# Sixteen weight tiles and eleven operand tiles begin at other places in a partition

## The chip, the cores and the metric

The kernel runs on one core of one Trainium2 chip. The metric is the device time of one execution in microseconds (us). A profiled execution also has a span, from its first to its last recorded instruction, and a trace of every instruction.

## What is computed

The inputs are q, k and v of shape 8 x 8 x 576 x 64 (batch, heads, sequence, head dimension), w_in (512 x 2048) and w_out (2048 x 512). q, k and v are float32; w_in and w_out arrive as 8-byte floats, which the kernel takes apart into two words.

```
q_s = softmax of q over the head dimension
k_s = softmax of k over the sequence
kv  = einsum('bhsd,bhse->bhde', k_s, v)
x   = einsum('bhsd,bhde->bhse', q_s, kv), heads put side by side: 4608 x 512
h   = x @ w_in
g   = h / (1 + exp(-1.702 h))
out = g @ w_out                                        4608 x 512, float32
```

## The kernel before

**Tiling.** The 4608 tokens are nine blocks of 512 (`t`, 0 to 8). For each block an attention part (`attend`) makes the block's x, transposed, with features on the partitions. A feed-forward part then goes through the 2048 hidden features in eight steps (`NS`) of two groups of 128 (`jj`); the pair `p` of groups goes up in even blocks and down in odd ones.

**Precision.** A matmul operand of the feed-forward part is kept as two float32r tiles, a high and a low part, and each product is three matmuls: high by high, high by low, low by high.

**First product, blocks 0 and 1** (`plain1`, line 795): for each step 24 matmuls of 512 columns, with `wj` (w_in) as the stationary operand and `xp` (x) as the moving one. **Blocks 2 to 8** (`ffn1`, line 842): seven products of six matmuls of 256 columns, in the order 6, 1, 2, 7, 5, 4, 3. They multiply sums of blocks of x (`xo`) by blocks of w_in (`wj`) or sums of these (`wt`); VectorE and ScalarE put the results together. That is 42 matmuls in a step. **Second product** (`ffn2`, line 905): 24 matmuls of 512 columns in a step, with the activated values `gh` and `gl` as the stationary operand and w_out (`w`) as the moving one, added up in four banks over the eight steps.

**Weights.** All sixteen tiles of w_out stay in SBUF from when they are converted (`load_w`, line 320, and `conv`, lines 329 to 369). Each of them is first the landing place (`raw`) of a piece of w_in, then of one of w_out, then holds the split w_out; four of them first hold v and q of block 0 (`early_tile`). w_in is split too and stored to memory (`kept`, `kept_t`), and from block 1 on GpSimd's DMA queue loads it back two steps ahead (`load_kept`, line 398): three DMAs a step, each issued when TensorE has read its buffer (`wj`, `wt`) for the last time. SP's queue carries everything else.

**Order.** `Plan` holds each piece of work with an engine, a cost and a rank, and writes out one fixed order per engine before anything runs. Costs and ranks don't depend on where a tile lies.

**Places.** All tiles come from one pool and lie one behind another in each partition in the order in which they are first named, behind a scratch for the descriptors of GpSimd's DMAs (16,384 bytes) and four constants of 32 bytes each. From the sizes it follows where a tile begins, in bytes modulo 512: `ident`, `kvn`, `g`, `gh`, `gl`, `tt`, `tmp` and `kt` at 128; the four `vt` (2,080 bytes each) at 128, 160, 192 and 224; `qt` and `qT` at 256; `wj`, `wide` and `wt` at 384; and, behind `first` with its 64 bytes, the sixteen tiles tagged `wo..` and the eleven tagged `place..` all at 448. Inside these tiles TensorE's operands begin at multiples of 512 from the tile's start, but those of `vt` (line 635) at multiples of 260. [...]

**The places of x.** Eleven tiles of 4 KB are shared: `xp` of block 0 is in 0 to 3 and of block 1 in 4 to 7; later `xf` is in 0 and 1, `xs` in 2 and 3, and `xo` of the products 7, 5, 4, 3, 6, 1, 2 in 4 to 10.

Of the kernel before, what the change touches and what calls it, by code (L numbers as in the profile page):

```python
# [9 lines left out]
F32 = mybir.dt.float32  # L10
F32R = mybir.dt.float32r
I32 = mybir.dt.int32
# [124 lines left out]
def efficient_attention_then_gelu_ffn(  # L137
# [27 lines left out]
    nc = tc.nc  # L165
    B, H, S, D = q.shape
    NTOK, DM = out.shape
    FF = w_out.shape[0]
    P = 128
    C = 4  # L170
# [6 lines left out]
    NS = NJ // 2  # L177
# [4 lines left out]
    SLOTS = 15  # L182
    Y, Z = 4, 5
    LATE = (0.0, 2.0, 6.0)

    const = ctx.enter_context(tc.tile_pool(name="const", bufs=1))
    psum = ctx.enter_context(tc.tile_pool(name="psum", bufs=1, space=bass.MemoryType.PSUM))
# [4 lines left out]

    def sb(name, shape, dtype=F32, tag=None):
        return const.tile(shape, dtype, name=name, tag=tag or name)

    ident = sb("ident", [P, P])
    kvn = [sb(f"kvn{i}", [P, NP, D]) for i in range(2)]
    gt = [[sb(f"g{i}{u}", [P, 2, HT]) for i in range(2 - u)] for u in range(2)]
    gs = [[sb(f"g{s}{i}", [P, 2, 2, HT], F32R) for i in range(2)] for s in "hl"]
    tt = sb("tt", [P, 4, HT])  # L200
# [27 lines left out]
    places = {}  # L228

    def place(n, name, shape, dtype=F32):  # L230
        if (n, name) not in places:
            places[n, name] = sb(f"{name}{n}", shape, dtype, tag=f"place{n}")
        return places[n, name]

    def xp(t, hp):
        return place(4 * t + hp, "xp", [P, 2, TB], F32R)

    def xf(half):
        return place(half, "xf", [P, 2, 2, HT])

    def xsum(n):
        return place(3 if n == 4 else 2, "xs", [P, 2, 2, HT])[:, n % 2]
# [63 lines left out]
    raws, wo = {}, {}  # L306

    def load_w(p, kind, rank):
        for jj in range(2):
            tag = f"wo{p}{jj}"  # L310

            def run(jj=jj, tag=tag, j=p + NS * jj):
                raw = raws[p, jj] = sb("raw", [P, 2 * DM], I32, tag=tag)
                if kind == "wi":
                    nc.sync.dma_start(
                        out=raw.rearrange("p (c f) -> p c f", c=KC),
                        in_=w_in[:, 2 * j * P : 2 * (j + 1) * P].rearrange("(c p) f -> p c f", p=P),
                    )
                else:
                    nc.sync.dma_start(out=raw, in_=w_out[j * P : (j + 1) * P, :])  # L320

            plan.add("SP", plan.ISSUE, (), (tag,), rank + 0.01 * jj, run, size=2 * DM * 4 * P)

    def words(raw):
        return raw.rearrange("p (f t) -> p f t", t=2)

    def high(f, w):

        nc.scalar.activation(f, w[:, :, 1].bitcast(F32), AF.Prelu, scale=2.0**-112, alpha=-(2.0**32))

    def narrow(f, w):

        fi = f.bitcast(I32)
        nc.vector.scalar_tensor_tensor(fi, fi, 3, w[:, :, 0], ALU.logical_shift_left, ALU.bitwise_or)

    def low(w):
        lo = w[:, :, 0].bitcast(U32)
        nc.vector.tensor_scalar(lo, lo, 29, None, ALU.logical_shift_right)  # L338
# [6 lines left out]
    def next_tmp(n):  # L345
        nt[n] += 1
        i = nt[n] % n
        return (tmp[i] if i < 2 else wide[:, i - 2]), ("tmp", i)

    def conv(p, kind, rank):  # L350

        for jj in range(2):
            ff, T = next_tmp(6)
            K = f"wo{p}{jj}"
            KD = K if kind == "wo" else ("wj", p % 2, jj)

            def w(jj=jj):
                return words(raws[p, jj])

            def dst(jj=jj):  # L360
                return wo[p, jj] if kind == "wo" else wj[p % 2][jj].rearrange("p s c f -> p s (c f)")

            def c5(jj=jj, ff=ff, tag=K, dst=dst):
                if kind == "wo":
                    wo[p, jj] = sb("w", [P, 2, DM], F32R, tag=tag)
                nc.scalar.copy(dst()[:, 0], ff)  # L366

            def c6(ff=ff, dst=dst):
                nc.vector.tensor_tensor(out=dst()[:, 1], in0=ff, in1=dst()[:, 0].bitcast(F32), op=ALU.subtract)  # L369

            plan.add("ACT", 0.66, (K,), (T,), rank, lambda ff=ff, w=w: high(ff, w()))
            plan.add("DVE", 0.38, (K,), (K,), rank, lambda w=w: low(w()))
            plan.add("DVE", 0.69, (K, T), (T,), rank, lambda ff=ff, w=w: narrow(ff, w()))
            plan.add("ACT", 0.62, (T,), (KD,), rank, c5)
            plan.add("DVE", 0.69, (KD, T), (KD,), rank, c6)
            if kind == "wi":

                def run_s(jj=jj):
                    nc.sync.dma_start(
                        out=kept[p][jj], in_=wj[p % 2][jj].bitcast(F32).rearrange("p s c f -> p (s c f)")  # L380
                    )

                plan.add("SP", plan.ISSUE, (KD,), (("kept", p, jj),), rank, run_s, size=2 * DM * P * 4)
# [72 lines left out]
    def late(t):  # L456

        return LATE[min(t, 2)]

# [23 lines left out]
    early = {}  # L483

    def early_tile(kind, hp):
        tag = f"wo{NS - 1 if kind == 'q' else NS - 2}{hp // 2}"
        if tag not in early:
            early[tag] = sb(f"early{tag}", [P, 2, 2, C * D], tag=tag)
        return early[tag][:, hp % 2].rearrange("p h (c d) -> p h c d", d=D), (("early", tag, hp % 2), tag)

    def load_v(b, hp, rank):
        if b == 0:
            x, K = early_tile("v", hp)
            src = v[b, 2 * hp : 2 * hp + 2, 0:SM, :]

            def run_e():
                nc.sync.dma_start(
                    out=x.rearrange("p h c d -> p h (c d)"), in_=src.rearrange("h (p c) d -> p h (c d)", c=CM)
                )

            plan.add("SP", plan.ISSUE, (), (K[0],), rank, run_e, size=2 * SM * D * 4)
            return

        def run():
            for h in range(2):
                nc.sync.dma_start(
                    out=vt[hp][:, h, :, 0:D], in_=v[b, 2 * hp + h, 0:SM, :].rearrange("(p c) d -> p c d", c=CM)
                )

        plan.add("SP", 2 * issue(b), (), (("vt", hp),), rank, run, size=3 * SM * D * 4, late=late(b))  # L510

    def load_q(t, hp, rank):
        runs = [(0, 1, 1), (1, 0, 1)] if hp % 2 else [(0, 0, 2)]
        x, K = early_tile("q", hp) if t == 0 else (None, (("qt", hp),))

        def run():
            for b, s0, p0, p1 in parts(t):
                for o, h, m in runs:
                    src = q[b, 2 * hp + h : 2 * hp + h + m, s0 : s0 + (p1 - p0) * C, :]
                    if t == 0:  # L520
                        nc.sync.dma_start(
                            out=x[p0:p1, o : o + m].rearrange("p h c d -> p h (c d)"),
                            in_=src.rearrange("h (p c) d -> p h (c d)", c=C),
                        )
                    else:
                        nc.sync.dma_start(
                            out=qt[hp][p0:p1, :, o : o + m], in_=src.rearrange("h (p c) d -> p c h d", c=C)
                        )

        plan.add(  # L530
            "SP", issue(t) * len(parts(t)) * len(runs), (), (K[0],), rank, run, size=(3 if t else 2) * TB * D * 4, late=late(t),
        )
# [81 lines left out]
    def kv_pairs(b, hps, t, rank):  # L614
# [5 lines left out]
        for hp in hps:  # L620
            reads += [("kt", hp), ("kl", hp), *(early_tile("v", hp)[1] if b == 0 else (("vt", hp),))]
# [383 lines left out]
```

## Time and profile before

| | |
|---|---|
| median of 2 runs | 851.38 us (851.37 to 851.38) |
| the profiled execution | 850.68 us, span 848.7 us |
| TensorE matmuls (PE) | 841.5 us busy, 99% of the span |
| TensorE weight loads (PEld) | 720.9 us, 85% |
| VectorE (DVE) | 520.8 us, 61% |
| ScalarE (ACT) | 496.5 us, 58% |
| GpSimd (POOL) | 116.4 us, 14% |
| DMA | 155.63 MB, mean 183 GB/s |

A matmul's record begins when the matmul begins and its end is modelled, so records of neighbours overlap: their mean length is not the pace. The pace is read from how far apart the beginnings lie, as the chain of waits does, whose pieces add up to the span. The row PEclk, the granted clock of TensorE in tenths of full speed, is 9 in all 40 slices of the page.

### The profile page before, as it was taken

To read this page: it belongs to the slowest core of one execution; us is meant where nothing else is said; L and a number is where in the kernel's file an instruction comes from. 1 tells how busy PE (TensorE), PEld (TensorE's weight loads), DVE (VectorE), ACT (ScalarE), POOL (GpSimd) and SP (SyncE) were. 2 spreads that over 40 slices of the span, in tenths; PEclk is the share of its full clock that TensorE was granted. 3 is DMA by queue.
4 is the path that set the end of the run, shared out by engine and by line. 5 is a ranking of instruction groups with operands and counts; after the bars stand their busy time and mean duration, and the time that the engine had idled before them with its cause. 6 is when DMAs were issued, how large, how long until landed. Compare 5 with 4: busy or idle time off the path is not lost.

```text
span 848.7 us, 14608 instructions
## 1 busy us (share of the span) xinstructions
PE 841.5 (99%) x5644; PEld 720.9 (85%) x5644; DVE 520.8 (61%) x1082; ACT 496.5 (58%) x839; POOL 116.4 (14%) x175
## 2 busy tenths in 40 slices
PE   9999999999999999999999999999999999999998
PEld 4687788778898898889988999899988998899996
DVE  8899995988637884456645674475357532453333
ACT  4798879769637667456744665564366533353222
POOL 1000021120114031110211021100110011101110
PEclk9999999999999999999999999999999999999999
DMA  9999935793469737564765476623664264416541
GB/s 289 287 347 353 265 133 190 238 327 151 134 213 234 216 81 230 163 196 112 230 191 147 131 210 186 174 88 124 194 182 122 68 210 150 145 50 199 174 149 51
DMA packets 127845, 155.63 MB, mean 183 GB/s; under 512 B 76576, under 2 KB 105760, under 8 KB 121376
## 3 DMA queue, kind: packets, MB, share of 16 engines
q0 software_dynamic: 25248, 83.37, 31.8%
q1 hardware_dynamic: 102528, 71.32, 28.4%
q8 instruction: 45, 0.74, 0.4%
q14 instruction: 24, 0.20, 0.1%
HBM read 128.45 MB, written 26.21 MB: 182 GB/s over the span
## 4 chain that ended last, share of the span: by engine, by line
PE 93%; DVE 3%; DMA 2%; ACT 1%; issue 1%; DVEq 0%
PE bank L905 44%; PE bank L842 33%; PE bank L795 8%; PE bank L635 2%; DMA raw<-in_moe_w_out 2%; PE bank L705 2%; PE bank L684 2%; PE bank L297 1%; PE bank L583 0%; PE bank L584 0%; DVE w L369 0%; DVE wj L369 0%; DVE gl L813 0%; DVE raw L338 0%; DVE kt L557 0%
## 5 line engine op out<-in xcount | busy, mean ns | idle before, releaser
L905 PE MATMUL bank<-w,gh 128*128 128x512 f32 x1152 | 359.3, 393 | 0.3 <-DVE w L369 0.3
L905 PE MATMUL bank<-w,gl 128*128 128x512 f32 x576 | 225.7, 392 | 0.0
L905 PEld LDWEIGHTS bank<-w,gh 128*128 128x128 f32 x1152 | 199.8, 188 | 30.2 <-DVE w L369 1.1
L842 PE MATMUL bank<-xo,wt 128*128 128x256 f32 x1344 | 187.6, 280 | 0.0
L842 PEld LDWEIGHTS bank<-xo,wt 128*128 128x128 f32 x1344 | 176.4, 188 | 11.0 <-DVE g L855 0.8
L842 PEld LDWEIGHTS bank<-xo,wj 128*128 128x128 f32 x1008 | 136.7, 188 | 12.2 <-issue 1.6
L842 PE MATMUL bank<-xo,wj 128*128 128x256 f32 x1008 | 145.7, 280 | 0.5 <-ACT tt L866 0.5
L858 ACT ACTIVATE g<-g 128x512 f32<-128x512 f32 x112 | 58.8, 525 | 142.6 <-DVE g L855 142.1
L905 PEld LDWEIGHTS bank<-w,gl 128*128 128x128 f32 x576 | 108.3, 188 | 24.0
L855 DVE TENSOR_TENSOR g<-bank,tt 128x256 f32<-128x256 f32 x168 | 70.7, 422 | 87.8 <-PE bank L842 87.5
L886 DVE TENSOR_TENSOR gl<-g,gh 128x512 fp32r<-128x512 f32 x112 | 77.2, 690 | 72.3 <-ACT gh L883 71.6
L855 DVE TENSOR_TENSOR tt<-bank,tt 128x256 f32<-128x256 f32 x112 | 47.3, 422 | 106.1 <-PE bank L842 88.8
L398 POOL DMA_DIRECT2D wj<-kept x96 | 59.4, 619 | 379.9 <-PE bank L842 321.4
L795 PE MATMUL bank<-xp,wj 128*128 128x512 f32 x384 | 100.6, 396 | 0.3 <-ACT wj L366 0.2
L795 PEld LDWEIGHTS bank<-xp,wj 128*128 128x128 f32 x384 | 71.0, 188 | 19.6 <-issue 2.6
L883 ACT CAST gh<-g 128x512 fp32r<-128x512 f32 x112 | 69.6, 621 | 3.2
L858 ACT ACTIVATE g<-bank 128x256 f32<-128x256 f32 x56 | 21.7, 387 | 73.5 <-PE bank L842 73.3
L546 POOL PARTITION_ALL_REDUCE mx<-mx x32 | 34.8, 1086 | 197.3 <-DVE mx L542 170.4
L398 POOL DMA_DIRECT2D wt<-kept_t x42 | 22.2, 530 | 124.0 <-PE bank L842 124.0
L858 ACT ACT_TABLE_LOAD x27 | 34.6, 1283 | 0.5
L665 ACT ACT_TABLE_LOAD x26 | 33.4, 1283 | 0.5
L866 ACT COPY tt<-bank 128x256 f32<-128x256 f32 x56 | 20.8, 371 | 19.1 <-PE bank L842 18.9
(103 smaller groups left out, 795.1 us busy)
## 6 DMA issues: line engine op xcount, KB each, us to landing
wt<-kept_t POOLq DMA_DIRECT2D x42, 1024.0 KB, 5.2
wj<-kept POOLq DMA_DIRECT2D x54, 512.0 KB, 3.7
wj<-kept POOLq DMA_DIRECT2D x42, 256.0 KB, 4.8
out<-tmp SPq DMA_DIRECT2D x36, 256.0 KB, 3.0
kt<-in_k SPq DMA_DIRECT2D x32, 256.0 KB, 4.0
raw<-in_moe_w_in SPq DMA_DIRECT2D x16, 512.0 KB, 8.2
raw<-in_moe_w_out SPq DMA_DIRECT2D x16, 512.0 KB, 7.4
kept<-wj SPq DMA_DIRECT2D x16, 512.0 KB, 7.1
```

Source lines behind the costliest of these rows:

```text
L398: "POOL", 1.0, (key,), (ring,), R(t, step - 2, off), lambda: nc.gpsimd.dma_start(out=out(), in_=src), size=size
L546: nc.gpsimd.partition_all_reduce(flat, flat, P, bass_isa.ReduceOp.max)
L635: nc.tensor.matmul(pk[r0 : r0 + D, m, cols], lhs, rhs, start=c == 0, stop=c == CM, tile_position=(0, r0))
L665: nc.scalar.activation(x, x, AF.Exp)
L795: nc.tensor.matmul(bank[bk], w[:, l, c, :], x[:, r], start=c == 0 and e == 0, stop=c == KC - 1 and e == 2)
L842: nc.tensor.matmul(ph[bk], w, x[:, r, c, :], start=opens and c == 0 and e == 0, stop=c == 1 and e == 2, skip_group_check=True,)
L855: return lambda: nc.vector.tensor_tensor(out=o, in0=ph[bk], in1=x, op=ALU.add)
L858: return lambda: nc.scalar.activation(o, x, AF.Gelu_apprx_sigmoid)
L866: vec("ACT", act(n), (ZB,), (A,), 2, lambda: nc.scalar.copy(a, ph[Z]))
L883: vec("ACT", act(2 * n), half, H, slot, lambda c=c, gh=gh: nc.scalar.copy(gh, c))
L886: nc.vector.tensor_tensor(out=gl, in0=c, in1=gh.bitcast(F32), op=ALU.subtract)
L905: nc.tensor.matmul(bank[c], l, r, start=first_ and e == 0, stop=last and e == 2)
```

## The change

`apart` allocates a tile with 512 bytes (128 words) more and returns the part of it that begins `off` bytes in. The sixteen tiles tagged `wo..` get the offsets 32 x (2p + jj), so 0, 32, ... 480; seven of the eleven places get those of `XAT`, and the other four 0, also with 512 bytes more. To make room, the scratch for the descriptors of GpSimd's DMAs is 2,048 bytes of each partition and not 16,384. No instruction is added or removed.

```diff
--- before.py
+++ after.py
@@ -182,6 +182,11 @@
     SLOTS = 15
     Y, Z = 4, 5
     LATE = (0.0, 2.0, 6.0)
+    XAT = {8: 480, 9: 64, 10: 192, 4: 464, 5: 32, 6: 416, 7: 496}
+
+    def wat(p, jj):
+        return 32 * (2 * p + jj)
+
 
     const = ctx.enter_context(tc.tile_pool(name="const", bufs=1))
     psum = ctx.enter_context(tc.tile_pool(name="psum", bufs=1, space=bass.MemoryType.PSUM))
@@ -192,6 +197,17 @@
 
     def sb(name, shape, dtype=F32, tag=None):
         return const.tile(shape, dtype, name=name, tag=tag or name)
+
+    def apart(name, shape, dtype, tag, off):
+        n = 1
+        for x in shape[1:]:
+            n *= x
+        t = const.tile([P, n + P], dtype, name=name, tag=tag)[:, off // 4 : off // 4 + n]
+        if len(shape) == 3:
+            return t.rearrange("p (a b) -> p a b", a=shape[1])
+        if len(shape) == 4:
+            return t.rearrange("p (a b c) -> p a b c", a=shape[1], b=shape[2])
+        return t
 
     ident = sb("ident", [P, P])
     kvn = [sb(f"kvn{i}", [P, NP, D]) for i in range(2)]
@@ -229,7 +245,7 @@
 
     def place(n, name, shape, dtype=F32):
         if (n, name) not in places:
-            places[n, name] = sb(f"{name}{n}", shape, dtype, tag=f"place{n}")
+            places[n, name] = apart(f"{name}{n}", shape, dtype, f"place{n}", XAT.get(n, 0))
         return places[n, name]
 
     def xp(t, hp):
@@ -310,7 +326,7 @@
             tag = f"wo{p}{jj}"
 
             def run(jj=jj, tag=tag, j=p + NS * jj):
-                raw = raws[p, jj] = sb("raw", [P, 2 * DM], I32, tag=tag)
+                raw = raws[p, jj] = apart("raw", [P, 2 * DM], I32, tag, wat(p, jj))
                 if kind == "wi":
                     nc.sync.dma_start(
                         out=raw.rearrange("p (c f) -> p c f", c=KC),
@@ -362,7 +378,7 @@
 
             def c5(jj=jj, ff=ff, tag=K, dst=dst):
                 if kind == "wo":
-                    wo[p, jj] = sb("w", [P, 2, DM], F32R, tag=tag)
+                    wo[p, jj] = apart("w", [P, 2, DM], F32R, tag, wat(p, jj))
                 nc.scalar.copy(dst()[:, 0], ff)
 
             def c6(ff=ff, dst=dst):
@@ -483,9 +499,10 @@
     early = {}
 
     def early_tile(kind, hp):
-        tag = f"wo{NS - 1 if kind == 'q' else NS - 2}{hp // 2}"
+        p_ = NS - 1 if kind == "q" else NS - 2
+        tag = f"wo{p_}{hp // 2}"
         if tag not in early:
-            early[tag] = sb(f"early{tag}", [P, 2, 2, C * D], tag=tag)
+            early[tag] = apart(f"early{tag}", [P, 2, 2, C * D], F32, tag, wat(p_, hp // 2))
         return early[tag][:, hp % 2].rearrange("p h (c d) -> p h c d", d=D), (("early", tag, hp % 2), tag)
 
     def load_v(b, hp, rank):
@@ -989,7 +1006,7 @@
     import concourse.bacc as bacc
     from concourse.bass_utils import run_bass_kernel_spmd
 
-    nc = bacc.Bacc("TRN2", target_bir_lowering=False, num_devices=1)
+    nc = bacc.Bacc("TRN2", target_bir_lowering=False, num_devices=1, dynamic_dma_scratch_size=2048)
     arrays, args = {}, []
     for name in _INS:
         a = np.ascontiguousarray(inputs[name])
```

## Rows read from the trace of the kernel before

**Rows 1.** Page, its first line and busy time of each engine.

```profile
span 848.7 us, 14608 instructions
...
PE 841.5 (99%) x5644; PEld 720.9 (85%) x5644; DVE 520.8 (61%) x1082; ACT 496.5 (58%) x839; POOL 116.4 (14%) x175
```

**Rows 2.** Page, the chain that ended last: share of the span by line.

```profile
PE bank L905 44%; PE bank L842 33%; PE bank L795 8%; PE bank L635 2%; DMA raw<-in_moe_w_out 2%; PE bank L705 2%; PE bank L684 2%; PE bank L297 1%; PE bank L583 0%; PE bank L584 0%; DVE w L369 0%; DVE wj L369 0%; DVE gl L813 0%; DVE raw L338 0%; DVE kt L557 0%
```

**Rows 3.** Groups by form: count | busy us, mean ns | idle before.

```profile
L905 PE MATMUL bank<-w,gh 128*128 128x512 f32 x1152 | 359.3, 393 | 0.3 <-DVE w L369 0.3
L905 PE MATMUL bank<-w,gl 128*128 128x512 f32 x576 | 225.7, 392 | 0.0
...
L795 PE MATMUL bank<-xp,wj 128*128 128x512 f32 x384 | 100.6, 396 | 0.3 <-ACT wj L366 0.2
```

**Rows 4.** Stretches: busy us (count) by engine, PEclk, DMA share, GB/s.

```profile
735.56:746.05 10.49, 10.49 (x68) 9.46 (x67) 3.13 (x8) 3.31 (x7) 0.00 (x0) 1.00 0.15 46
...
819.51:830.00 10.49, 10.49 (x67) 9.45 (x67) 3.40 (x8) 3.05 (x6) 0.00 (x0) 1.00 0.15 45
412.98:423.25 10.27, 10.27 (x67) 9.27 (x67) 4.11 (x10) 10.07 (x18) 1.79 (x3) 1.00 0.89 271
```

**Rows 5.** Chain in order of time, 395 to 424 us: start, us, what.

```profile
412.98 2.07 PE bank L905 x9
415.05 1.36 PE bank L842 x12
```

**Rows 6.** Chain in order of time, 768 to 792 us.

```profile
779.61 1.41 PE bank L842 x12
```

**Rows 7.** Line 842: duration ns min/median/max, first and last start us.

```profile
L842 PE MATMUL bank<-xo,wt x1344: 276/279/388, 216.7 to 836.0; 128*128 128x256 f32 x192
...
L842 PE MATMUL bank<-xo,wj x1008: 276/279/393, 218.1 to 838.1; 128*128 128x256 f32 x168
```

**Rows 8.** Chain, the longest pieces of the whole span.

```profile
32.42 7.97 DMA raw<-in_moe_w_out
67.53 9.65 DMA raw<-in_moe_w_out
...
99.29 2.06 PE bank L795 x9
101.35 2.06 PE bank L905 x9
```

**Rows 9.** TensorE in order of time, 569 to 571.1 us: start, us, group.

```profile
569.77 0.64 PE L635 MATMUL bank<-vt,kt 128*64 128x65 f32 x16
...
570.36 0.64 PE L635 MATMUL bank<-vt,kt 128*64 128x65 f32 x16
```

**Rows 10.** DMA issues: KB each, median us from issue to landing.

```profile
raw<-in_moe_w_out SPq DMA_DIRECT2D x16, 512.0 KB, 7.4
...
vt<-in_v SPq DMA_DIRECT2D x56, 128.0 KB, 4.3
...
kl<-in_k SPq DMA_DIRECT2D x8, 128.0 KB, 3.1
vl<-in_v SPq DMA_DIRECT2D x8, 128.0 KB, 5.1
...
qt<-in_q SPq DMA_DIRECT2D x8, 128.0 KB, 4.4
```

**Rows 11.** Line 398, GpSimd's DMAs: duration, waits, landing.

```profile
L398 POOL DMA_DIRECT2D wj<-kept x96: 527/558/716, 127.3 to 817.7; - x96
L398 POOL DMA_DIRECT2D wt<-kept_t x42: 528/528/546, 226.2 to 815.6; - x42
...
who waited for it (us, times):
...
DMA to landing us min/median/max: 3.4/4.9/9.8
```

**Rows 12.** DMA queues: packets, MB, share of 16 engines.

```profile
q0 software_dynamic: 25248, 83.37, 31.8%
```

## The prediction, made before the changed kernel had run

> **What bounds the kernel now.** I read the page's busy times first, then the chain that ended last, then TensorE's groups, and then stretches of single steps. TensorE is busy 841.5 of 848.7 us and GpSimd 14% [rows 1]. Lines 905, 842 and 795, the three matmul lines of the feed-forward part, hold 85% of the chain [rows 2]. They are 1728 matmuls of 512 columns at line 905, 384 of 512 at line 795 [rows 3] and 1344 + 1008 = 2352 of 256 at line 842 [rows 7]. So nothing moves the end unless it changes the pace of these matmuls or makes TensorE wait.
>
> The pace has two levels. From block 2 on, one step is 42 matmuls at line 842 and 24 at line 905, and there are 2352 / 42 = 56 steps. [...] Twelve at line 842 take 1.36 us in the short step [rows 5] and 1.41 us in the long one [rows 6], that is 113.3 and 117.5 ns each. The records of line 842 last 276 ns at the least and 279 at the median [rows 7], so more than half of them are of the slower kind. Nine of 512 columns take 2.06 to 2.07 us, 229 ns each [rows 5, 8].
>
> [...]
>
> **The change part by part.** The sum is made against the profiled execution, 850.68 us with its span of 848.7; the median of the runs shown is 851.38, so 0.7 us is to be added.
>
> *Instructions.* None is added, removed or reordered: `apart` allocates 512 bytes more and slices. Cost 0. The 27 padded tiles take 27 x 512 = 13,824 bytes of each partition and the scratch gives back 14,336, which is 28 x 512. So all other tiles keep their starts modulo 512.
>
> *Starts that TensorE reads.* Before, every moving operand of the three lines begins at 448, the stationary ones at 128 (`gh`, `gl`) or 384 (`wj`, `wt`). After, the sixteen w_out tiles begin at all the multiples of 32, and the x operands of blocks 2 to 8 at 416, 0, 128, 400, 480, 352 and 432. The trace speaks against any effect. In block 0 nine matmuls of line 795, whose operands begin 64 apart, take 2.06 us, and the nine of line 905 right behind them, 320 apart, take 2.06 too [rows 8]. At line 635 the value tiles begin 32 bytes further from pair to pair, and sixteen matmuls take 0.64 us for one pair and for the next [rows 9]. Neither settles it: the first two distances differ by just 256, and line 635 moves 65 columns of plain float32. The bounds come from the two paces. If every step ran like the short one, at most 56 x 0.22 = 12.3 us would go, and at least half of it, 6.2, since more than half are slow. If every step ran like the long one, at most 6.2 us would come. I take -1.5: any shift of timing may draw the paces of the steps anew, and half and half would give back only what is slow above half now; that value is near 0 and the bound of 6.2 is far.
>
> [...]
>
> *Starts that the other engines use.* ScalarE and VectorE write or read the moved tiles, 496.5 and 520.8 us busy in all [rows 1]. Behind TensorE they have room in every later step: 3 us of 10.5 at the end [rows 4]. I cost it at 0. In the first 80 us, where they stand on the chain, a slower one would show.
>
> *DMAs into the moved tiles.* w_out loads stand on the chain twice, 7.97 and 9.65 us [rows 8], and land in 7.4 us at the median [rows 10]. Half of them now begin off a multiple of 64 bytes. The nearest rows are two loads of 128 KB in 256-byte pieces: into `vt`, whose pieces lie 260 bytes apart and so begin at all sorts of places, 4.3 us; into `qt`, at multiples of 256, 4.4 us [rows 10]. So 0. The far end is `vl` against `kl`, again 260 apart and not, 5.1 against 3.1 us, though `vl` is issued behind `kl` [rows 10]: two pieces on the chain by 2 us each, +4.
>
> *GpSimd's scratch.* 96 + 42 = 138 DMAs go through it, issued in 0.53 to 0.72 us and landing in 4.9 us at the median and 9.8 at the most; the list of who waited for them is empty [rows 11]. They are 25,248 packets [rows 12], 183 each. A smaller scratch could hold an issue back until an earlier DMA has landed. By the order of the products the last reload of a step has over one step, 10.3 us, until its buffer is read again, so one extra landing of 4.9 us is covered at no cost. Where two landings add up, about 10 us meet 10 us, and TensorE waits now and then: up to +0.2 us in each of 56 steps, +11. I take 0, since a step has three of these DMAs and GpSimd is busy for 14% of the span [rows 1].
>
> [...]
>
> *Sum:* 850.7 + 0 - 1.5 + 0 + 0 + 0 = 849.2 us; with the 0.7, 849.9. I say 849.5, its own range 844 to 856.
>
> **The rivals.** *All steps go fast.* If the starts set which pace a step falls into, spread starts could end the bad one. For: the two paces hold for many steps on end, whatever else runs. Against: the equal nines of rows 8. Time: 851 less 6 to 12, about 841. Chance 0.18.
>
> *The whole loss goes.* [...] Chance 0.06, a part of the win included. [...]
>
> *Odd starts cost a beat (slower).* [...] Chance 0.10.
>
> *The scratch or the loads bite.* The +4 and +11 above: 855 to 862. Chance 0.06.
>
> **How the numbers follow.** The forecast keeps 0.60. The range, 838 to 861, takes in the forecast, the fast rival to its bound (851 - 12.3) and most of the last one; outside lie 0.06 below and 0.10 above with the tails. [...] Faster 0.07, same 0.87, slower 0.06.
>
> **What would show it.** In the changed profile: twelve matmuls at line 842 at 1.36 or 1.41 us, nine at line 905 at 2.06, and steps of 10.27 or 10.49 mean the forecast holds, and the mix of the two is the whole difference. [...] w_out landing in more than 8 us, or GpSimd's DMAs named as what TensorE waits for, shows the last. A new pace that is neither of the two, better or worse, is what would make me wrong.

## The result: slower, and outside the range

The changed kernel takes 861.22 us (860.85 to 861.59) against 851.38: a ratio of 1.0116, 95% interval 1.0072 to 1.0159. The loss is under the 2% that divides slower from the same, but the interval leaves no room for no change. The forecast was 849.5 with a range of 838 to 861. The rows of the change bear line numbers that are higher by 16 or 17: 922 is the old 905, 859 the old 842, 812 the old 795, 336 the old 320.

The page after, busy times and DMA issues:

```profile
span 859.0 us, 14608 instructions
...
PE 850.4 (99%) x5644; PEld 725.6 (84%) x5644; DVE 522.0 (61%) x1082; ACT 497.6 (58%) x839; POOL 116.6 (14%) x175
...
wt<-kept_t POOLq DMA_DIRECT2D x42, 1024.0 KB, 5.2
...
raw<-in_moe_w_out SPq DMA_DIRECT2D x16, 512.0 KB, 7.3
```

The span is longer by 10.3 us and TensorE is busy for 8.9 us more [rows 1]. VectorE and ScalarE gained 1 us each, the w_out loads land as before [rows 10], and the number of instructions is the same. To see where the time went, landmarks of the chain are laid side by side: start, us, what. Before:

```profile
218.98 2.76 PE bank L905 x12
...
838.38 3.46 PE bank L905 x15
```

and after:

```profile
67.68 9.90 DMA raw<-in_moe_w_out
101.92 2.09 PE bank L922 x9
110.99 2.10 PE bank L812 x9
...
220.94 2.78 PE bank L922 x12
...
848.59 3.49 PE bank L922 x15
```

At the second w_out load on the chain the two are still 0.15 us apart [rows 8]. By the twelve matmuls near 220 us, 1.96 us have gone, by the last fifteen 10.21. So 8.25 us were lost in the 56 steps between, 0.15 a step, and 1.8 in blocks 0 and 1. Nine matmuls take 2.09 to 2.10 us where they took 2.06 [rows 8].

The same two stretches of steps, busy time by engine, PEclk, DMA share:

```profile
417.43:428.00 10.57, 10.57 (x68) 9.48 (x67) 4.17 (x9) 10.37 (x18) 1.79 (x3) 1.00 0.89 267
787.35:797.91 10.56, 10.56 (x67) 9.48 (x67) 3.39 (x8) 3.06 (x6) 1.79 (x3) 1.00 0.55 175
```

The first is the work of the old step at 412.98 us, which took 10.27 [rows 4], with the other engines as busy as then. The short step is gone, and the long one of 10.49 has become 10.56. TensorE waits in neither. The pieces of the chain inside show how:

```profile
787.35 2.10 PE bank L922 x9
789.45 1.43 PE bank L859 x12
...
797.91 2.09 PE bank L922 x9
800.00 1.43 PE bank L859 x12
```

Twelve matmuls of 256 columns take 1.43 us, more than either of the old paces, 1.36 [rows 5] and 1.41 [rows 6]. Of the 143 groups of just twelve such matmuls in the whole kernel, 42 took 1.36 us before and none does now, by the beginnings in the two traces. Over the whole kernel, the mean time between the beginnings of one matmul and the next, with gaps over 250 and 130 ns left out as waits, went from 229.5 to 232.2 ns for 512 columns and from 116.3 to 118.4 for 256. With 2112 and 2352 of them that is 5.7 + 4.8 = 10.5 us, as much as the span grew by (10.3). The waits of TensorE that the trace lists make up 3.1 us before and 4.3 after. So the loss lies in the pace of the feed-forward matmuls, and more than half of it in those of 512 columns.

### The profile page after: what moved, and what is told of

Same layout as the page of the kernel before. It is cut to its first block, busy times and chain, and to the rows that moved or that the text cites. A ratio compares the mean times of both kernels' runs of the same rounds, so it can differ in the third digit from the quotient of the medians.

```text
span 859.0 us, 14608 instructions
## 1 busy us (share of the span) xinstructions
PE 850.4 (99%) x5644; PEld 725.6 (84%) x5644; DVE 522.0 (61%) x1082; ACT 497.6 (58%) x839; POOL 116.6 (14%) x175
## 4 chain that ended last, share of the span: by engine, by line
PE 92%; DVE 3%; DMA 3%; ACT 1%; issue 0%; SPq 0%; DVEq 0%
PE bank L922 44%; PE bank L859 33%; PE bank L812 8%; PE bank L652 2%; DMA raw<-in_moe_w_out 2%; PE bank L722 2%; PE bank L701 2%; PE bank L313 1%; PE bank L600 0%; PE bank L601 0%; DMA qt<-in_q 0%; DVE gl L830 0%; DVE wide L350 0%; DVE w L385 0%; DVE wj L385 0%
## 5 line engine op out<-in xcount | busy, mean ns | idle before, releaser
L859 PE MATMUL bank<-xo,wt 128*128 128x256 f32 x1344 | 190.4, 282 | 0.0
L859 PEld LDWEIGHTS bank<-xo,wt 128*128 128x128 f32 x1344 | 178.9, 188 | 11.3 <-issue 1.8
L859 PE MATMUL bank<-xo,wj 128*128 128x256 f32 x1008 | 147.6, 282 | 0.5 <-ACT tt L883 0.5
```

Source lines behind the costliest of these rows:

```text
L859: nc.tensor.matmul(ph[bk], w, x[:, r, c, :], start=opens and c == 0 and e == 0, stop=c == 1 and e == 2, skip_group_check=True,)
```

## Experiments

Three theories were left. *Odd starts*: a start off a multiple of 64 bytes costs. *Distance*: what counts is how far the moving operand's start lies from the stationary one's. *Mixing*: starts that change from matmul to matmul cost, whatever they are. Each edit is against the changed kernel. The ratios are to the kernel before, measured anew beside each group of runs (851.6 to 852.1 us).

**Room alone.** Padding and the small scratch, all starts as before.

```diff
-    XAT = {8: 480, 9: 64, 10: 192, 4: 464, 5: 32, 6: 416, 7: 496}
+    XAT = {}
-        return 32 * (2 * p + jj)
+        return 0
```

> The padding and the 2 KB scratch alone, every start as before. Starts theory (the 10 us come from where the moving operands begin): about 851 us, nine matmuls of the w_out line in 2.06 us. Scratch theory (GpSimd's smaller scratch or the padding costs): about 861 us with the same nine at 2.06 to 2.09.

Measured 851.84 us, ratio 0.9997 (0.9982 to 1.0012). No cost of the scratch and the padding is seen, so the loss comes from the starts.

**One set at a time.** w_out with its starts and `XAT = {}`; then x's operands with theirs and `return 0`.

> Only the sixteen w_out tiles get their starts, x's operands stay at 448. If each operand pays for its own start, the 512-column matmuls carry 2.7 ns more each (232.2 against 229.5 ns between beginnings in the changed kernel), so about +4.7 us for 1728 of them: 856. If the loss needs both sets moved (jumps between w_out and x), clearly less than half of 10: 853 or under.

> Only x's operands get their starts, w_out stays at 448. If each operand pays for its own start, the 256-column matmuls carry 2.0 ns more each (118.4 against 116.3): +4.8 us for 2352, about 856. If the loss needs both: 853 or under.

Measured 857.38 us, ratio 1.0061 (1.0038 to 1.0084), and 857.58, ratio 1.0073 (1.0050 to 1.0096). Each set pays for itself: w_out's starts alone bring the 512-column pace to 231.7 ns and leave the other at 116.5; x's alone bring the 256-column pace to 118.4 and leave the other at 230.1. The two losses add up to 1.34%, the change has 1.16%. But this does not hold matmul by matmul. In the first of these kernels two of the sixteen w_out tiles still lie as far from the stationary operand as before, modulo 256 bytes, and their matmuls take 231.5 ns where the same tiles took 229.5 in the kernel before.

**Everything 32 bytes on, or only what moves.** In the first kernel a tile of 32 bytes stands ahead of all others, so moving and stationary operands shift together; in the second only the w_out and x tiles shift. In both, every moving operand begins at 480.

```diff
-    XAT = {8: 480, 9: 64, 10: 192, 4: 464, 5: 32, 6: 416, 7: 496}
+    XAT = {}
-        return 32 * (2 * p + jj)
+        return 0
...
+    sb("front", [P, 8])
     ident = sb("ident", [P, P])
```

> Every tile, the stationary ones too, begins 32 bytes later: moving operands at 480, stationary at 160 and 416, the distance between them as before. Odd starts theory (a start off a multiple of 64 costs): all of them are off, +10 to +28 us, 861 to 879. Distance theory (what counts is how far the moving start lies from the stationary one) and mixing theory (what counts is that starts change from matmul to matmul): 851.

```diff
-    XAT = {8: 480, 9: 64, 10: 192, 4: 464, 5: 32, 6: 416, 7: 496}
+    XAT = {n: 32 for n in range(11)}
-        return 32 * (2 * p + jj)
+        return 32
```

> All w_out and x tiles at +32 (480), stationary operands where they were: the distance to them is 96 modulo 256 and no longer 64. Odd starts theory: as with all tiles moved by 32, +10 to +28 us. Distance theory: the w_out tiles that begin at 224 or 480 in the changed kernel take 233.9 ns a matmul and the x tile at 480 119.2; for all matmuls that is 2112 x 4.4 + 2352 x 2.9 ns = +16 us, about 867. Mixing theory: 851, since all starts are the same.

Measured 852.96 us, ratio 1.0009 (0.9996 to 1.0021), and 867.8, ratio 1.0176 (1.0153 to 1.0199). This pair decides. Pieces of the chain where all tiles are shifted, from an early and from a late stretch (here line 923 is the old 905 and 860 the old 842):

```profile
417.93 1.36 PE bank L860 x12
...
436.38 2.06 PE bank L923 x9
...
790.02 2.07 PE bank L923 x9
792.10 1.41 PE bank L860 x12
```

and where only the moving operands are:

```profile
784.80 2.10 PE bank L922 x9
786.90 1.44 PE bank L859 x12
...
795.44 2.10 PE bank L922 x9
```

The first has both old paces, the second a worse one, with the same moving starts. So odd starts cost nothing that is seen, and neither mixing nor any property of the moving start by itself explains the second, whose starts are all alike. What differs is how far the moving operands lie from the tiles that stayed. These are not the stationary operands alone, and no run moved those alone. The other tiles belong to the other engines and to DMAs, though, or to the matmuls of the attention part. For 256-column matmuls with no instruction of VectorE, ScalarE or GpSimd and no DMA packet within 0.1 us, the two traces give 116.5 ns (119 of them) and 119.5 (127): the difference is there without them. So the distance to the stationary operand is what is left.

**Other distances.** The same edit with 64, 128, 192, 256 and 16 in place of 32.

> All w_out and x tiles at +64 (0 modulo 512), distance 128. Odd starts theory and mixing theory: 851. Distance theory: w_out tiles at 0 or 256 took 232.5 ns and the x tile at 0 117.9 in the changed kernel, so 2112 x 3.0 + 2352 x 1.6 = +10 us, about 861.

> All at +128 (64 modulo 512), distance 192. Odd starts and mixing: 851. Distance theory: w_out tiles at 64 or 320 took 232.0 ns, +5 us for the 512-column matmuls; no x tile lay there, so 851 to 862, not below 851 unless this distance suits the 256-column ones.

> All at +192 (128 modulo 512), distance 0. Odd starts and mixing: 851. Distance theory: w_out tiles at 128 or 384 took 230.5 ns and the x tile at 128 118.7 in the changed kernel: 2112 x 1.0 + 2352 x 2.3 = +7.5 us, about 859.

> All w_out and x tiles at +256 (192 modulo 512): the distance to the stationary operands changes by 256. If only the distance modulo 256 counts, 852 us and the old paces (226, 229, 232 ns for 512 columns, 113 or 118 for 256). If it counts modulo 512, as the shifts of 32 to 192 did: 855 to 868.

> All at +16 (464), distance 80: does a quarter of 64 bytes count? If the distance counts in 16-byte steps, somewhere between the old kernel and the +32 one (852 and 868), about 860. If it counts in pieces of 32 or 64 bytes: 852, or 868 as the +32 one.

All of them in one table. The distance is the moving start less the stationary one, modulo 256; the paces are mean times between beginnings as above, of one profiled execution each:

```
shift   distance   us      ratio (interval)            512 columns   256 columns
  0       64       851.8   0.9997 (0.9982 to 1.0012)     229.6 ns      116.5 ns
 16       80       862.7   1.0121 (1.0101 to 1.0141)     231.2         119.6
 32       96       867.8   1.0176 (1.0153 to 1.0199)     233.5         119.8
 64      128       860.9   1.0102 (1.0085 to 1.0120)     232.8         118.6
128      192       855.3   1.0037 (1.0026 to 1.0048)     232.7         115.2
192        0       859.0   1.0079 (1.0060 to 1.0098)     229.7         119.1
256       64       851.9   0.9998 (0.9987 to 1.0009)     229.6         116.3
```

For the shifts of 32, 64 and 192 the distance theory had forecast about 867, 861 and 859. The shift of 256, the only one tried that long, gives the old kernel back, with 41 of 143 twelves at 1.36 us and the others as below, and nothing was seen to depend on more than the distance modulo 256:

```profile
789.05 1.41 PE bank L859 x12
790.47 2.07 PE bank L922 x9
```

A shift of 64, which keeps every start on a multiple of 64, costs 1%, and 16 bytes cost 1.2%. The chain with 16, 64 and 192:

```profile
788.65 2.08 PE bank L922 x9
790.73 1.44 PE bank L859 x12
```

```profile
786.55 2.10 PE bank L922 x9
788.65 1.42 PE bank L859 x12
```

```profile
784.87 2.07 PE bank L922 x9
786.93 1.43 PE bank L859 x12
```

**Two ways to gain.** At distance 192 the 256-column matmuls are faster than in the old kernel, 115.2 ns against 116.3. So x's operands of blocks 1 to 8 were put there, and w_out left at 64; and, since the x tile at distance 32 had the best pace of the seven in the changed kernel, 116.9 ns, x was put at 32. The first edit follows; the other has 224 in place of 128.

```diff
-    XAT = {8: 480, 9: 64, 10: 192, 4: 464, 5: 32, 6: 416, 7: 496}
+    XAT = {n: 128 for n in range(4, 11)}
-        return 32 * (2 * p + jj)
+        return 0
```

> x's operands of blocks 1 to 8 at +128 (64), w_out as before at 448. With all tiles at +128 the 256-column matmuls took 115.15 ns against 116.34, the 512-column ones 232.7 against 229.5. If each matmul's pace hangs on its own distance: 2352 x -1.2 ns = -2.8 us and +0.6 for the 192 matmuls of block 1, so about 850, a little faster than before. If changes of distance from matmul to matmul cost by themselves (mixing): 853 or more.

> x's operands of blocks 1 to 8 at +224 (160), distance 32 modulo 256, w_out as before. In the changed kernel the x tile at this distance had the best pace of all seven, 116.9 ns, among neighbours at other distances. If that was its distance's doing, 116.9 or less for all, so 850 to 853; if not, 117.9 to 119.3 like the others, 856 to 859.

Measured 857.3 us, ratio 1.0060 (1.0042 to 1.0077), and 854.84, ratio 1.0036 (1.0024 to 1.0048). The first is a miss for the distance theory taken matmul by matmul, which gave 850; it lies where changes of distance from matmul to matmul were said to cost by themselves. With all w_out and x tiles shifted by 128 most twelves take 1.36 or 1.37 us:

```profile
783.04 2.09 PE bank L922 x9
785.13 1.37 PE bank L859 x12
...
787.89 1.36 PE bank L859 x12
```

With x alone at the same distance every full twelve in the same stretch takes 1.41:

```profile
784.31 2.08 PE bank L922 x9
786.38 1.41 PE bank L859 x12
...
789.18 1.41 PE bank L859 x12
```

The 256-column pace is 117.2 ns there and not 115.2, and the 512-column pace went up to 231.0 though w_out did not move. So the distance of a matmul is not all. Mixing is refuted as the only cause, but mixed distances cost here too, as they did for the two w_out tiles above: what the matmuls around it do seems to count, and no run shows how. The second fell between what its two cases gave, at 117.4 ns, and tells little. No kernel tried beats the old one; the three that tie with it (room alone, everything 32 bytes on, the shift of 256) are those with its distances modulo 256.

## Why the prediction was wrong

**Where to look: right.** That only the matmuls' own pace could move the end held: the loss between beginnings, 10.5 us, is the loss of the kernel. The prediction's last sentence also named what it would look like: a new pace that is neither of the two.

**Scratch, loads, other engines: right.** Costed at 0. Room alone gives 0.9997; w_out lands in 7.3 us; between 424 and 850 us the chain has no piece of VectorE or ScalarE. That a smaller scratch holds an issue back was not seen: GpSimd's DMAs are issued in 0.53 to 0.73 us and land in 4.8 at the median, against 0.53 to 0.72 and 4.9 before [rows 11], and none of TensorE's waits names them.

**The step that failed** is "Starts that TensorE reads". It said that the trace speaks against any effect and set the bounds by the two paces seen, steps of 10.27 and of 10.49 us [rows 4]: "If every step ran like the long one, at most 6.2 us would come." The term, taken as -1.5, measured about +10, beyond that bound, because new distances brought paces that the old kernel doesn't have: in the changed kernel twelve matmuls in 1.43 us, and nine of 512 columns in 2.09 to 2.10. For the 512 columns the prediction knew one pace only, 229 ns, and they brought 5.7 of the 10.5 us. Two paces of one kernel are not the ends of what a pace can be when all feed-forward matmuls of that kernel ran at one distance modulo 256. That the time lies just 0.2 us above the range is no near hit: the upper end stood for a scratch or loads that bite, and these cost nothing. The two rivals that foresaw a gain had the wrong sign.

**The evidence that misled.** The equal nines of [rows 8] lie at distances 64 and 320. The text noted that these differ by just 256, and then counted them against a rival all the same. The shift of 256 shows that they are one and the same case. The equal groups of [rows 9] did vary the distance, by 32 bytes from pair to pair. But they are matmuls of 65 columns of plain float32 with 64 stationary columns; that they don't react says nothing of the float32r ones. Why they don't was not tried.

**The odd starts rival** was right that the kernel gets slower, by luck. With every feed-forward operand at an odd start, all tiles shifted by 32, no loss is seen: 852.96 us, ratio 1.0009. With a shift of 64, which keeps every feed-forward start on a multiple of 64, it is there: 860.9, 1.0102. The shift of 32 for the moving operands alone, with its twelves at 1.44 us and +1.8%, would fit a price on odd starts just as well; a threshold in time alone could not tell the two apart.

**Prices without a run.** No run shows a price of an odd start, which the chance of 0.10 and the +10 to +28 us of two expectations supposed; the runs showed the 1.0009 above in its place. Nor does one show the win behind the chance of 0.06 that the whole loss goes: the fastest means of a kernel are 115.2 and 229.5 ns, and the fastest twelves take 1.36 us, 113.3 ns each.

**What stays open.** Where all feed-forward matmuls share one distance modulo 256, the runs show a pace for each of six, 115.2 to 119.8 ns and 229.6 to 233.5, and the old one again after 256 bytes (116.3 and 229.6). They don't show what in the memory or in TensorE makes it so, nor what a matmul at another distance does to its neighbours. Nor do they show how a run of matmuls falls into the faster or the slower pace at one distance: the old kernel, and the one with all tiles shifted, have both 1.36 and 1.41 for the same work.

## What to carry to other kernels

What follows is shown for this one kernel. Its float32r matmuls run back to back, each with a weight load (5644 of both in the whole kernel [rows 1]). In a kernel like it, keep one distance modulo 256 bytes between the moving and the stationary operand's start, and try several: here 64 was the best of six for the whole kernel, and the six lie within 1.8%. Spreading the starts gave up the good distance for good and bad ones, and in the spread of w_out even the two tiles at the good distance were slower, 231.5 ns against 229.5. When a trace seems to show that something has no effect, ask whether any of its rows varied that thing for the instructions that count.

## What was not expected of the hardware

- The pace of TensorE changed with how far the moving operand's start lies from the stationary one's in a partition: 229.6 to 233.5 ns for 512 columns and 115.2 to 119.8 for 256 in the seven kernels of the table. It was no wait and no lower clock: in the changed kernel's steps shown TensorE is busy for 10.57 of 10.57 us and 10.56 of 10.56 at a granted clock of 1.00, and with the shift of 32 a step has 10.64 of 10.64 at 1.00.
- The two sizes were fastest at different distances: for 512 columns 64 and 0 (229.6 and 229.7 ns), for 256 columns 192 (115.2).
- The pace did not follow what the other engines did: two of the changed kernel's steps take 10.57 us with the DMA engines 0.89 busy and ScalarE 10.37 us, and 10.56 us with 0.55 and 3.06.
